# Decode attention on one core: 54 K and V loads moved from SyncE's to GpSimd's queue

## The chip, the cores and the metric

The kernel runs on one core of a Trainium2 chip. The metric is the device time of one execution in microseconds (us), as the median of several runs. The chip's parts go by the profile's names: PE (TensorE, the matrix engine), DVE (VectorE), ACT (ScalarE), POOL (GpSimd) and SP (SyncE, which computes nothing and here issues DMAs). 16 DMA engines move data between the chip's memory and the 128 partitions of the core's own memory.

## The reference

One decoding step of a transformer block for two sequences: layer norm, attention over a cache of 8192 positions with 32 heads of 128, and a gated feed-forward layer, all in bf16.

```python
def _A_ref(x, k_cache, v_cache, wq, wo):      # x: 2 x 1 x 512; caches: 2 x 32 x 8192 x 128
    q = (x @ wq).reshape(B, Sq, Hq, Dh).transpose(0, 2, 1, 3)
    scores = einsum("bhqd,bhkd->bhqk", q, k) * (Dh ** -0.5)
    o = einsum("bhqk,bhkd->bhqd", softmax(scores), v)
    return o.transpose(0, 2, 1, 3).reshape(B, Sq, Hq * Dh) @ wo

def _B_ref(x, W_gate, W_up, W_down):          # F = 1376
    gate, up = x @ W_gate, x @ W_up
    return ((gate * (gate > 0)) * up) @ W_down

h = x + _A_ref(_layernorm(x), k_cache, v_cache, wq, wo)
out = h + _B_ref(_layernorm(h), W_gate, W_up, W_down)
```

Each query meets each key once, so nothing of the caches is used twice: 2 x 2 x 32 x 8192 x 128 elements of 2 B are 268 MB that have to be read.

## The kernel before

**Tiles and steps.** The 64 pairs of sequence and head are worked through two heads at a time, in N = 32 steps. For one step, K of two heads is one tile of 128 partitions by 16,384 elements (ROW; 32 KB a partition, 4 MB in all), and V another. Each partition holds 128 positions (NT) of 128 elements, which lie one after the other in the chip's memory, so that a load is 128 rows of 32 KB, eight for each DMA engine. There are two buffers for K (the halves of kbuf, called kh) and two for V (vbuf); step i uses buffer i % 2 of each.

**A step.** `scores(i)` multiplies K by the query in place on DVE (L358), adds each product row up by halving (L383) and a last reduction (L387), and takes the largest score of each partition (L395), which PE spreads (L397). `powers(i)` runs inside the next step: DVE reduces the largest score (L312) and ACT takes the exponentials into pgz (L315). `values(i)`, also inside the next step, multiplies V by them on PE, two matmuls written out (L408) and the other thirty in a loop that PE runs by itself (L434, L440). ACT collects the result (L450), and PE turns four steps' results at a time (L459).

**Loads.** `load_kv(cache, buf, i, pieces)` issues the load of step i at L144. At the start SP issues, in this order, the weights wq, K of step 0 in four pieces, K of step 1 (K1 below) and V of step 0 (V0). From then on each `scores(i)` with i from 1 to 30 issues K of step i + 1 and then V of step i, behind a `tc.no_sync_barrier()` that sets the order of the plan and waits for nothing by itself. A K load waits until `scores(i - 1)` has read the buffer, a V load until `values(i - 2)` has. SP issues them in order and waits in order. V of step 31, the weights wo, W_gate, W_up and W_down follow on SP as well. The argument `single_packet` asks for all rows that an engine gets of one load to be framed as one packet; before, it is set for i from 1 to 27 (TOGETHER is N - 4 = 28).

**Order.** For four engines the order of instructions is as written; for POOL it is made by a planner:

```python
    ORDERED = {getattr(mybir.EngineType, e) for e in ("PE", "DVE", "Activation", "SP")}
    with tc.manual_schedule(engines=ORDERED):
```

POOL only sets up constants at the start (L174 to L204, the selects through a helper at L151): memsets and selects of ident, pick, nscale, fold, part, quarter, sel, rest and quot. It issues no DMA.

**The end.** Behind the last step come the output projection (L535), the layer norm and the feed-forward layer (L571, L604), and a store of the result (L618).

Of the kernel before, what the change touches and what calls it, by code (L numbers as in the profile page):

```python
# [18 lines left out]
def _dram(t, offset, dims):  # L19
    return bass.AP(tensor=t.tensor, offset=t.offset + offset, ap=[list(d) for d in dims])  # L20
# [3 lines left out]
def kernel(  # L24
# [13 lines left out]
    nc = tc.nc  # L38
# [58 lines left out]
    kh = [kbuf[:, s, :] for s in range(2)]  # L97
# [38 lines left out]
    TOGETHER = N - 4  # L136
# [3 lines left out]
    def load_kv(cache, buf, i, pieces=1):  # L140
        b, g = steps[i]
        w = ROW // pieces
        for k in range(pieces):
            nc.sync.dma_start(  # L144
                out=buf[i % 2][:, k * w:(k + 1) * w],
                in_=_dram(cache, (b * Hkv + 2 * g) * Sk * Dh + k * w, [[ROW, P], [1, w]]),
                single_packet=0 < i < TOGETHER,
            )

    def select(t, fill, base, pattern, mult, op=ALU.not_equal):  # L150
# [13 lines left out]
    with tc.manual_schedule(engines=ORDERED):  # L164

        nc.sync.dma_start(out=wq_all, in_=_dram(A_wq, 0, [[KC * Hq * Dh, P], [1, KC * Hq * Dh]]))  # L166
        for b in range(B):
            nc.scalar.dma_start(out=xrow[b:b + 1, :], in_=_dram(A_x, b * D, [[D, 1], [1, D]]))
        load_kv(A_k_cache, kh, 0, pieces=4)
        load_kv(A_k_cache, kh, 1)  # L170
        load_kv(A_v_cache, vbuf, 0)

        masks.make_identity(nc, ident)
# [473 lines left out]
```

## Time and profile before

| | |
|---|---|
| median of three runs | 659.18 us (659.13 to 659.39) |
| profiled execution | 657.6 us, its span from the first to the last instruction; the profile gives no other time of it |
| busy: PE, DVE, ACT, POOL | 398.7, 607.9, 67.0, 7.9 us |
| DMA | 281.26 MB in 11379 packets, mean 428 GB/s |
| SP's queue (q1) | 11360 packets, 281.06 MB, 99.3% of 16 engines' span |
| first multiply of DVE (L358) | starts at 23.24 us |
| V of step 31 | issued at 614.44 us, landed at 634.45 us |
| last weights | landed at 654.18 us |

How to read it: the page divides the span into 40 slices and gives the busy share of each in tenths; "DMA share" in a table by windows is the mean busy share of the 16 DMA engines. A line of DMA issues gives the KB of one load and the median us from its issue to its landing. In a timeline, "idle before <-releaser" is what the engine waited for. "SPq" is an instruction of SP's queue, "L144" a line of the kernel. Below the page's views the trace keeps a record of each DMA packet, with queue, start, duration and bytes; a packet there is one row of a load, or a 4 B record that ends a load on one engine.

### The profile page before, as it was taken

To read this page: it belongs to the slowest core of one execution; us is meant where nothing else is said; L and a number is where in the kernel's file an instruction comes from. 1 tells how busy PE (TensorE), PEld (TensorE's weight loads), DVE (VectorE), ACT (ScalarE), POOL (GpSimd) and SP (SyncE) were. 2 spreads that over 40 slices of the span, in tenths; PEclk is the share of its full clock that TensorE was granted. 3 is DMA by queue.
4 is the path that set the end of the run, shared out by engine and by line. 5 is a ranking of instruction groups with operands and counts; after the bars stand their busy time and mean duration, and the time that the engine had idled before them with its cause. 6 is when DMAs were issued, how large, how long until landed. Compare 5 with 4: busy or idle time off the path is not lost.

```text
span 657.6 us, 7128 instructions
## 1 busy us (share of the span) xinstructions
PE 398.7 (61%) x1647; PEld 129.5 (20%) x1647; DVE 607.9 (92%) x290; ACT 67.0 (10%) x200; POOL 7.9 (1%) x51
## 2 busy tenths in 40 slices
PE   2127666666676555657666556775556665565496
PEld 1002111211121111211112111121112111121256
DVE  0899999999999999999999999999999999999941
ACT  2110111110000000000000000000000000000220
POOL 4000000000000000000000000000000000000000
PEclk9999788798887777898887789767778876779885
DMA  8999999999999999999999999999999999999997
GB/s 359 439 444 421 442 433 427 444 415 446 427 434 433 427 442 425 440 434 427 440 424 441 429 435 432 429 440 424 440 431 432 438 423 441 432 433 436 425 422 298
DMA packets 11379, 281.26 MB, mean 428 GB/s; under 512 B 1282, under 2 KB 1380, under 8 KB 2020
## 3 DMA queue, kind: packets, MB, share of 16 engines
q1 hardware_dynamic: 11360, 281.06, 99.3%
q8 instruction: 9, 0.15, 0.1%
q14 instruction: 6, 0.05, 0.0%
q10 hardware_dynamic: 4, 0.00, 0.0%
HBM read 281.05 MB, written 0.00 MB: 427 GB/s over the span
## 4 chain that ended last, share of the span: by engine, by line
DVE 61%; DMA 36%; PE 1%; issue 1%; SPq 0%; ACT 0%; DVEq 0%; ACTq 0%
DMA kbuf<-in_A_k_cache_dram 30%; DVE kbuf L358 28%; DVE kbuf L383 27%; DVE scol L387 4%; DMA vbuf<-in_A_v_cache_dram 3%; DMA kbuf<-in_B_W_down_dram 3%; PE po L408 1%; DVE nm L312 1%; DVE pm L395 0%; SPq L144 0%; ACT pgz L315 0%; PE d_ps L604 0%; SPq L166 0%; DVE rz L297 0%; PE y_ps L612 0%
## 5 line engine op out<-in xcount | busy, mean ns | idle before, releaser
L440 PE MATMUL po<-vbuf,pgz 128*8 x870 | 300.1, 443 | 68.0 <-issue 66.7
L358 DVE TENSOR_TENSOR kbuf<-kbuf,qrep 128x16384 bf16<-128x16384 bf16 (+2 forms) x33 | 277.1, 8398 | 10.2 <-DMA kbuf<-in_A_k_cache_dram 9.8
L383 DVE TENSOR_TENSOR kbuf<-kbuf 128x8192 bf16<-128x8192 bf16 (+4 forms) x128 | 274.5, 2144 | 3.3
L440 PEld LDWEIGHTS po<-vbuf,pgz 128*8 x870 | 79.9, 92 | 299.1 <-issue 263.9
L408 PE MATMUL po<-vbuf,pgz 128*8 128x512 bf16 x122 | 47.0, 521 | 135.4 <-PEq L434 111.3
L450 ACT ACTIVATE ob<-po 8x512 f32<-8x512 f32 x31 | 18.2, 586 | 436.5 <-PEq L434 427.3
L387 DVE TENSOR_REDUCE scol<-kbuf 128x128 f32<-128x1024 bf16 (+1 forms) x32 | 38.8, 1214 | 1.2
L315 ACT ACTIVATE pgz<-scol,nm 64x128 bf16<-64x128 f32 x64 | 28.0, 438 | 85.4 <-DVE nm L312 84.5
L397 PE MATMUL mx_ps<-nscale,pm 128*128 128x128 f32 x64 | 15.0, 317 | 29.7 <-DVE pm L395 19.0
L408 PEld LDWEIGHTS po<-vbuf,pgz 128*8 128x8 bf16 x58 | 2.7, 84 | 130.4 <-issue 130.4
L397 PEld LDWEIGHTS mx_ps<-nscale,pm 128*128 128x128 f32 x64 | 9.7, 190 | 39.6 <-issue 19.3
L234 PE MATMUL q_ps<-wbig,xn 128*2 128x512 bf16 x32 | 10.7, 469 | 3.0 <-DMA wbig<-in_A_wq_dram 3.0
L315 ACT ACTIVATION_READ_ACCUMULATOR pgz<-scol,nm 64x1 f32 x64 | 11.7, 184 | 0.0
L312 DVE TENSOR_REDUCE nm<-mx_ps 128x2 f32<-128x128 f32 x32 | 9.1, 284 | 1.4 <-PE mx_ps L397 1.4
L408 PEld LDWEIGHTS <-pgz 128*8 128x8 bf16 x64 | 6.1, 98 | 21.3 <-ACT pgz L315 10.0
L395 DVE TENSOR_REDUCE pm<-scol 128x1 f32<-128x128 f32 x32 | 9.1, 286 | 1.1
L459 PE MATMUL o_ps<-sel,ob 128*128 128x8 f32 (+1 forms) x64 | 8.7, 262 | 0.1
L459 PEld LDWEIGHTS o_ps<-sel,ob 128*128 128x128 f32 x64 | 8.0, 197 | 1.4 <-ACT ob L450 1.2
L215 DVE COPY xc<-x_ps 128x8 f32<-128x8 f32 x1 | 0.2, 167 | 8.4 <-PE x_ps L211 8.4
L238 ACT ACTIVATE qrow<-q_ps 2x512 bf16<-2x512 f32 x8 | 4.7, 587 | 29.5 <-PE q_ps L234 29.5
L242 PE MATMUL r_ps<-qrow,pick 2*64 2x256 bf16 x32 | 3.9, 321 | 5.4 <-ACT qrow L238 5.4
L297 DVE RECIPROCAL rz<-o_ps 128x32 f32<-128x32 f32 (+3 forms) x4 | 1.0, 254 | 5.8 <-PE o_ps L289 4.6
(93 smaller groups left out, 75.5 us busy)
## 6 DMA issues: line engine op xcount, KB each, us to landing
vbuf<-in_A_v_cache_dram SPq DMA_DIRECT2D x32, 4096.0 KB, 23.4
kbuf<-in_A_k_cache_dram SPq DMA_DIRECT2D x31, 4096.0 KB, 19.8
wbig<-in_A_wq_dram SPq DMA_DIRECT2D x1, 4096.0 KB, 12.6
kbuf<-in_A_k_cache_dram SPq DMA_DIRECT2D x4, 1024.0 KB, 17.5
wbig<-in_A_wo_dram SPq DMA_DIRECT2D x1, 2048.0 KB, 24.5
wbig<-in_A_wo_dram SPq DMA_DIRECT2D x2, 1024.0 KB, 26.4
kbuf<-in_B_W_gate_dram SPq DMA_DIRECT2D x1, 1376.0 KB, 31.2
kbuf<-in_B_W_up_dram SPq DMA_DIRECT2D x1, 1376.0 KB
```

Source lines behind the costliest of these rows:

```text
L234: nc.tensor.matmul(out=q_ps[0:B, :], lhsT=xn[:, c, :], rhs=wq_sb[:, c, n * 512:(n + 1) * 512], start=(c == 0), stop=(c == KC - 1),)
L312: nc.vector.tensor_reduce(out=nm, in_=mx_ps, axis=AXIS.X, op=ALU.min)
L315: nc.scalar.activation(out=_free(pgz[s][r, :], j, [[2, NT]]), in_=scol[r, :], func=ACT.Exp, scale=SCALE, bias=nm[r, j:j + 1], accum_out=zc ...
L358: nc.vector.tensor_tensor(out=kv, in0=kv, in1=_free(qrep, (b * NG + g) * Dh, [[0, n], [1, Dh]]), op=ALU.mult,)
L383: nc.vector.tensor_tensor(out=lo, in0=lo, in1=_free(kt, half, [[Dh, nv], [1, half]]), op=ALU.add,)
L387: nc.vector.tensor_reduce(out=scol[:, 0:nv], in_=_free(kt, 0, [[Dh, nv], [1, 8]]), axis=AXIS.X, op=ALU.add,)
L395: nc.vector.tensor_reduce(out=pm, in_=scol, axis=AXIS.X, op=ALU.max)
L397: nc.tensor.matmul(out=mx_ps.rearrange("p a b -> p (a b)"), lhsT=_free(pm, 0, [[0, P]]), rhs=nscale, start=True, stop=True,)
L408: nc.tensor.matmul(out=made[i][0:2 * T4, :], lhsT=pgz[s][:, u * 2 * T4:(u + 1) * 2 * T4], rhs=vbuf[s][:, u * T4 * Dh:(u + 1) * T4 * Dh], s ...
L440: nc.tensor.matmul(out=made[i][0:2 * T4, :], lhsT=pgz[s][:, bass.ds((w * LOOP + u) * (2 * T4), 2 * T4)], rhs=vbuf[s][:, bass.ds((w * LOOP ...
L450: nc.scalar.activation(out=ob[32 * k:32 * k + 2 * T4, :], in_=made.pop(i)[0:2 * T4, :], func=ACT.Copy,)
L459: nc.tensor.matmul(out=o_of(i)[:, 0, 2 * g0:2 * (g0 + n)], lhsT=ob[:, t * Dh:(t + 1) * Dh], rhs=sel[:, t, 0:n, :], start=(t == 0), stop=(t ...
```

## The change

54 of the 64 loads of K and V go to POOL's queue: K of steps 2 to 28 and V of steps 1 to 27. They are the ones with `single_packet` set. The others stay on SP without it: all loads issued at the start, K of steps 29 to 31, V of steps 28 to 31, and all weights. So K1 loses the flag and K28 gains it. Nothing else is changed; buffers, waits and sizes are the same.

```diff
     def load_kv(cache, buf, i, pieces=1):
         b, g = steps[i]
         w = ROW // pieces
+        first = 2 if buf is kh else 1
+        many = first <= i < first + TOGETHER - 1
+        eng = nc.gpsimd if many else nc.sync
         for k in range(pieces):
-            nc.sync.dma_start(
+            eng.dma_start(
                 out=buf[i % 2][:, k * w:(k + 1) * w],
                 in_=_dram(cache, (b * Hkv + 2 * g) * Sk * Dh + k * w, [[ROW, P], [1, w]]),
-                single_packet=0 < i < TOGETHER,
+                single_packet=many,
             )
```

## The prediction

> **What bounds the kernel now.** I read the page first: the busy shares and slices, the queues, the chain that ended last; then the windows by stage, DVE's waits, the SP queue's issues, and last the trace's records of single DMA packets.
>
> ```profile
> DMA  8999999999999999999999999999999999999997
> GB/s 359 439 444 421 442 433 427 444 415 446 427 434 433 427 442 425 440 434 427 440 424 441 429 435 432 429 440 424 440 431 432 438 423 441 432 433 436 425 422 298
> ...
> q1 hardware_dynamic: 11360, 281.06, 99.3%
> ...
> DVE 61%; DMA 36%; PE 1%; issue 1%; SPq 0%; ACT 0%; DVEq 0%; ACTq 0%
> ...
> vbuf<-in_A_v_cache_dram SPq DMA_DIRECT2D x32, 4096.0 KB, 23.4
> kbuf<-in_A_k_cache_dram SPq DMA_DIRECT2D x31, 4096.0 KB, 19.8
> ```
>
> The 16 DMA engines are busy from the first slice to the last, nearly all of it on SP's one queue. The chain's "DVE 61%" must not mislead: up to 247 us DVE works through what the first loads gave it, and after that it waits for K at each step:
>
> ```profile
> core 0: us, PE busy (x) PEld busy (x) DVE busy (x) ACT busy (x) POOL busy (x), PEclk, DMA share, GB/s
> 0.00:43.00 43.00, 9.57 (x34) 3.70 (x34) 25.15 (x16) 6.62 (x10) 7.88 (x51) 1.00 0.98 411
> 43.00:247.00 204.00, 132.12 (x422) 37.98 (x422) 202.12 (x88) 22.69 (x65) 0.00 (x0) 0.85 1.00 432
> 247.00:595.00 348.00, 215.72 (x661) 63.12 (x660) 340.90 (x146) 28.27 (x90) 0.00 (x0) 0.81 1.00 433
> ```
>
> DMA share 1.00 at 432 to 433 GB/s in both middle stages: only a faster packet stream can shorten them. The packet records say how fast it is. Each load is eight rows of 32,768 B per engine; on one engine's sequence, rows follow at 1.2094 us, with 0.006 us more for a record of 4 B that ends the load: 9.681 us, for nearly each of 63 loads. The 8,192 B rows of K's first load follow at 0.3059 us. So 24,576 B more take 0.9035 us, 27.20 B per ns; at that rate 32,768 B need 1.2047 us, and **4.7 ns per row are a fixed cost of each packet**. K1 (flagged as one packet) and V0 (not flagged) both take 9.681 us, so on SP's queue the flag buys nothing.
>
> The cover of an issue is what still runs ahead of it:
>
> ```profile
> start us, us, engine line op out<-in xcount [idle before <-releaser]
> 265.95 0.33 SPq L144 DMA_DIRECT2D kbuf<-in_A_k_cache_dram  x1
> 271.71 0.33 SPq L144 DMA_DIRECT2D vbuf<-in_A_v_cache_dram  x1
> 285.19 0.33 SPq L144 DMA_DIRECT2D kbuf<-in_A_k_cache_dram  x1
> 290.94 0.33 SPq L144 DMA_DIRECT2D vbuf<-in_A_v_cache_dram  x1
> ```
>
> The K load issued at 285.19 has its last row at 305.11, 19.92 us later, of which 9.68 are its own: 10.2 us of work lay ahead of it. The same subtraction over all K and V loads issued from 37.7 us on gives at least 5.35 us (K2, at 37.71), about 10 for K and 14 for V later.
>
> **The change part by part.**
>
> *Issues.* 54 issues of 0.33 to 0.43 us leave SP and 54 appear on POOL, which works only in the first 9.5 us. No issue of POOL is in this trace; the nearest row is SP's 0.33, the far end the 8.1 us for which PE waited on ACT's x loads, but that is transfer in the opening burst and not issue. I bound it at 0.3 to 8 us and take about 1, near SP's row. Anything below 5.35 us is hidden by the rows ahead: cost 0; at 8 us the first loads would come late by up to 2.7 us, once, since from 247 us on K has 10 ahead of it. On POOL, as on SP, a V load queues behind the K load ahead of it, which waits for DVE; nothing else stands behind them there. SP then has K29 and V28 next, whose buffers come free later than those of K28 and V27, so it passes nothing early. The weights follow V31 as now.
>
> *The flag.* K1 loses it and K28 gains it; on SP its worth is 0 (K1 against V0, above).
>
> *Two queues at once.* At 37.7 us K2 on POOL meets V0's last 5.35 us on SP; near 556 us K29 on SP meets V27 on POOL. Work is only reordered. At worst V0 ends behind K2, at 52.7 instead of 43.1 us; its first use is at 49.0 us, so PE starts 4 us late, and V2, which had 9.2 us ahead of it, still has 5. Cost 0; without that cover it would be those 4 us, once.
>
> *The rows themselves.* Here lies the only gain there can be. If GpSimd's queue does frame eight rows as one packet, seven of eight fixed costs go: 7 x 4.7 = 33 ns a load, x 54 = 1.78 us, all on the path, since each load is. Bounds: 0 (as on SP) to all eight and the record at the end, 8 x 4.7 + 6 = 44 ns, x 54 = 2.35 us; below nothing if the queue is worse (rivals). I take 1.78, because that is what one packet for eight rows means. The Trainium skill (DMA: Bandwidth & Descriptors, "Why small descriptors are slow") puts about 3 cycles on each packet, which joining packets saves, and a further 32 B of metadata on each descriptor, which it doesn't; as an estimate that leaves 1.3 us of the 1.78. No run so far shows the split.
>
> *Sum*, against the profiled execution: span 657.6 - 1.8 = 655.8. The three timed runs have a median of 659.18, 1.5 us above that span; the same 1.5 us put the forecast at **657.4 us**, 0.27% faster. A measurement of this kernel tells about 0.2%, or 1.3 us, from no change.
>
> **The rivals.**
>
> *No difference (659.2).* The packet cost stays per row, as SP's flagged loads show it today, and the engines have no idle time to give back. For it: K1 = V0 to the nanosecond. Against: it is another queue. The Trainium skill (same page, "Issuing engines are not separate DMA queues") says that all queues end in the same 16 engines and that issuing from several only saves issue time; by that rule it would be this case, and the busy share of 1.00 agrees with it.
>
> *Slower: the stream loses its perfect packing.* Place: the 54 loads. SP's stream has no gap at all between loads, so GpSimd's can only equal it or be worse there; it decides from 1.32 / 54 = 24 ns a load. Price by the nearest row: if rows are cut to the 8,192 B that K0 has, three more fixed costs a row, 3 x 4.7 x 8 = 113 ns a load, x 54 = 6.1 us: 665.3. Cut in two it would be 2.0 us, 661.2. A stall per load of the kind the trace has where another queue's packet comes between (a row of 1.68 instead of 1.21 us) would be 0.47 x 54 = 25 us, the far end. The Trainium skill (same page, "Measured (HBM→SBUF, 128 partitions, SWDGE, issued from GpSimd)") lists 425 GB/s at 16 MB; at that rate, as an estimate, 54 loads would cost 10 us more.
>
> *Slower: POOL's order.* POOL's instructions are not held in written order, as those of PE, DVE, ACT and SP are; the start shows it, where the memset of quot (written last) precedes the selects of fold:
>
> ```profile
> 3.44 0.10 POOL L186 MEMSET fold<- 128x8 f32 x1
> ...
> 3.68 0.10 POOL L203 MEMSET quot<- 128x4 bf16 x1
> 3.73 0.19 POOL L151 TENSOR_SCALAR_AFFINE_SELECT fold<-fold 128x8 f32<-128x8 f32 x1
> ```
>
> V1's buffer is free from the start. Put ahead of K2, V1 would share the engines with K0, and DVE would start up to 9.7 us late. Then K3 is asked for at 66.4 us, the stream having run dry at 62.4; with about 2 us from issue to first row (the first load: 0.81 to 2.76) 6.0 us are lost for good: 665.2. If V stood ahead of K all the way, K would wait 5.8 us for V's release each step and then behind V's 9.7: some 5 us a step, over 100 us. Against both: a barrier in the source puts the pair behind the earlier step, K first.
>
> *Slower: DVE.* A step's DVE work is 18.8 to 19.0 us of 19.36; 0.34 us to spare. One us more per step over 27 steps would cost about 0.7 x 27 = 18 us, some 677. Nothing in the trace has POOL at work beside DVE's loop. The Trainium skill (SBUF — State Buffer, "Who interferes with whom") says that DVE in a two-port mode keeps GpSimd from writing descriptors, but that tensor_tensor and tensor_reduce did not, and the loop has only these two.
>
> **How the numbers follow.** Forecast 0.40; no difference 0.22; lost packing 0.22; POOL's order 0.10; DVE 0.06. The first is faster, the second the same, the other three slower: 0.38. The range starts at 656.7, just under the largest gain (659.18 - 2.35 = 656.8), and reaches to 667 over both 665 cases; outside are the stall per load, V ahead of K, and a slower DVE. Within the forecast alone it is 656.8 to 657.9.
>
> **What would show it.** Right: a second queue with 54 loads of 4 MB; rows in it at about 1.205 us and loads at 9.65; DMA share still 1.00; K waits of DVE as small as now; V31 landing some 1.8 us earlier than 634.45. No difference: 9.68 again. Lost packing: loads over 9.71 us, or DMA share under 1.00 in the middle stages. POOL's order: first DVE multiply later than 23.24, or V1 issued ahead of K2. DVE: L358 or L383 longer than 8.69 and 4.34 us. The forecast is wrong if loads on GpSimd's queue take 9.68 us or more.

## The result, and the profile after

The changed kernel takes 661.1 us (median of 7 runs, 660.9 to 661.7) against 659.18 us: a ratio of 1.0031, interval 1.0021 to 1.0042. It is 1.9 us slower, where 1.8 us faster was forecast. The profiled execution took 661.43 us with a span of 659.7 us, 2.1 us longer than the span before.

First the page of the changed kernel: the two queues (packets, MB, share of 16 engines' span), the chain by engine, and the issues with KB and median us to landing.

```profile
q0 software_dynamic: 7776, 226.50, 79.6%
q1 hardware_dynamic: 3584, 54.56, 19.4%
...
DVE 7%; PE 3%; issue 0%; DVEq 0%
...
kbuf<-in_A_k_cache_dram POOLq DMA_DIRECT2D x27, 4096.0 KB, 18.5
vbuf<-in_A_v_cache_dram POOLq DMA_DIRECT2D x27, 4096.0 KB, 22.1
```

54 loads are on a queue of their own, as meant. The chain that ended last has changed its kind: it holds only DVE and PE, and it can be followed back only to 589.4 us. Before, its last long wait was the one for the last weights, which landed at 654.18 us. The table by windows shows that the stream itself lost nothing in the middle:

```profile
core 0: us, PE busy (x) PEld busy (x) DVE busy (x) ACT busy (x) POOL busy (x), PEclk, DMA share, GB/s
43.00:247.00 204.00, 130.31 (x418) 37.73 (x418) 201.31 (x87) 22.64 (x65) 10.56 (x20) 0.86 1.00 432
247.00:595.00 348.00, 212.77 (x651) 63.03 (x652) 336.69 (x144) 28.21 (x90) 16.88 (x32) 0.81 1.00 433
```

Share and rate are those of before to the last digit, and the last row of all weights ends at 654.27 instead of 653.93 us. What differs is DVE: 336.7 instead of 340.9 us busy in the second stage. It stood still once. First PE's start on V27, before and after, then DVE's timeline at step 29, before and after:

```profile
568.02 1.01 PE L408 MATMUL po<-vbuf,pgz 128*8 128x512 bf16 x2 [5.14 <-PEq L434]
```

```profile
575.82 1.01 PE L411 MATMUL po<-vbuf,pgz 128*8 128x512 bf16 x2 [11.87 <-DMA kbuf<-in_A_k_cache_dram]
```

```profile
576.37 8.69 DVE L358 TENSOR_TENSOR kbuf<-kbuf,qrep 128x16384 bf16<-128x16384 bf16 x1 [0.25 <-DMA kbuf<-in_A_k_cache_dram]
584.98 0.28 DVE L312 TENSOR_REDUCE nm<-mx_ps 128x2 f32<-128x128 f32 x1
```

```profile
576.74 8.69 DVE L361 TENSOR_TENSOR kbuf<-kbuf,qrep 128x16384 bf16<-128x16384 bf16 x1 [0.25 <-DMA kbuf<-in_A_k_cache_dram]
590.06 0.29 DVE L315 TENSOR_REDUCE nm<-mx_ps 128x2 f32<-128x128 f32 x1 [4.62 <-PE mx_ps L400]
```

PE starts on V27 at 575.82 instead of 568.02 us. The spread of the next maxima (L400) stands behind these matmuls on PE, so DVE's reduction of them waits 4.62 us; before, it did not wait. V27 is late because its load took 30.2 us from issue to landing, where V loads on this queue take 22.1: it landed at 574.3 us, in the kernel before at 566.7, so 7.6 us late. (The wait names a DMA into kbuf, but PE starts 1.5 us after V27's landing, and before it was 1.4 us; what fills that time the trace does not show.) The packet records of one DMA engine tell why. P is a row of V27 on GpSimd's queue, S a row of K29 on SP's, with its start in us:

```
558.22P 559.43P 560.63S 561.84P 563.05S 564.26P 565.47S 566.68P 567.89S 569.10P 570.31S 571.52P 572.73S
```

K29 was issued on SP at 556.84, and its first row on any engine starts at 560.38. From then on each engine gives the queues one row each in turn, although the loads on GpSimd's queue carry single_packet. On this engine five rows of K29 come between those of V27, 6.0 us, and a sixth comes ahead of the record that ends V27's load, another 1.2 us; the rest of the 7.6 us is that the load before it, K28, already landed 0.4 us later. The engines move as much as before; but on one queue all of V27 would have gone first.

How 7.6 us become about 2: PE's spread comes at 589.56 instead of 581.76 us, but before it had been done 2.8 us ahead of the reduction, so DVE is 5.1 us late there. DVE starts its multiply of step 31 at 619.80 instead of 615.10 us (4.7 late), the store is issued at 656.64 instead of 655.44 (1.2 late, since the end of the kernel before spent the rest waiting for weights), and from the store's issue to the end of the span it is 3.1 instead of 2.2 us. So 1.2 us of the profiled 2.1 lie ahead of the store and 0.9 behind it.

### The profile page after: what moved, and what is told of

Its sections match the earlier page's. It is cut to its first block, busy times and chain, and to the rows that moved or that the text cites. A ratio compares the mean times of both kernels' runs of the same rounds, so it can differ in the third digit from the quotient of the medians.

```text
span 659.7 us, 7239 instructions
## 1 busy us (share of the span) xinstructions
PE 398.7 (60%) x1647; PEld 130.1 (20%) x1647; DVE 607.6 (92%) x290; ACT 66.9 (10%) x200; POOL 36.5 (6%) x105
## 3 DMA queue, kind: packets, MB, share of 16 engines
q0 software_dynamic: 7776, 226.50, 79.6%
## 5 line engine op out<-in xcount | busy, mean ns | idle before, releaser
L147 POOL DMA_DIRECT2D kbuf<-in_A_k_cache_dram x27 | 14.4, 534 | 352.4 <-DVE scol L390 311.1
L400 PE MATMUL mx_ps<-nscale,pm 128*128 128x128 f32 x64 | 15.0, 317 | 29.9 <-DVE pm L398 18.8
L147 POOL DMA_DIRECT2D vbuf<-in_A_v_cache_dram x27 | 14.2, 528 | 154.1 <-PEq L437 154.1
L400 PEld LDWEIGHTS mx_ps<-nscale,pm 128*128 128x128 f32 x64 | 9.7, 191 | 39.7 <-PEq L437 19.6
## 6 DMA issues: line engine op xcount, KB each, us to landing
vbuf<-in_A_v_cache_dram POOLq DMA_DIRECT2D x27, 4096.0 KB, 22.1
```

Of the source, the lines that this page charges most:

```text
L147: eng.dma_start(out=buf[i % 2][:, k * w:(k + 1) * w], in_=_dram(cache, (b * Hkv + 2 * g) * Sk * Dh + k * w, [[ROW, P], [1, w]]), single_pa ...
L400: nc.tensor.matmul(out=mx_ps.rearrange("p a b -> p (a b)"), lhsT=_free(pm, 0, [[0, P]]), rhs=nscale, start=True, stop=True,)
```

## The experiments

Theory H says that the time is lost at the handover, where SP takes the loads over while GpSimd's queue still has one to finish; theory Q that each load on GpSimd's queue costs something. Ratios are against the kernel before.

**No handover (e1).** All loads of the loop and the weights go to GpSimd's queue in the old order, and `keep_in_program_order` holds them on POOL in the order as written. The last pair of lines is that of wo; those of W_gate, W_up and W_down are changed in the same way.

```diff
+    def pooled(**kw):
+        tc.keep_in_program_order(nc.gpsimd.dma_start(**kw))
...
-        many = first <= i < first + TOGETHER - 1
-        eng = nc.gpsimd if many else nc.sync
+        many = first <= i
...
-            eng.dma_start(
+            (pooled if many else nc.sync.dma_start)(
...
-                    nc.sync.dma_start(
+                    pooled(
```

> Every load from K2 and V1 on, the weights behind V31 too, goes to GpSimd's queue in the order of before; SP keeps only the opening loads and the store. Theory H (handover): the 1.9 us are lost where the two queues share the engines row by row, when K29 on SP meets V27 on GpSimd's queue at 561 us; with no such meeting the time is that of before, 659.2 us (659.0 to 659.6), and V31 is issued near 614.4 us again. Theory Q (the queue): each load on GpSimd's queue costs 1.92 / 54 = 36 ns; 60 K and V loads and the weights would give 661.3 us or more.

Measured: 659.6 us, ratio 1.0006 (0.9997 to 1.0015). DVE is back in time at step 31:

```profile
615.11 7.62 DVE L363 TENSOR_TENSOR kbuf<-kbuf,qrep 128x14336 bf16<-128x14336 bf16 x1 [0.24 <-DMA kbuf<-in_A_k_cache_dram]
```

So with 93.1% of the stream on GpSimd's queue, where the changed kernel has 79.6%, the loss ahead of the store is gone: the store is issued at 655.40, before at 655.44. Q's 661.3 is out.

**An earlier handover (e2).** V13 meets K15 at about 290 us.

```diff
-        many = first <= i < first + TOGETHER - 1
+        many = first <= i < first + 13
```

> GpSimd's queue keeps only K2 to K14 and V1 to V13; the handover to SP comes at about 290 us. Theory H: V13 lands some 7 us late there, DVE waits once for 4 to 5 us about a step later, and wins back 0.34 us per step in the 16 steps that follow, 5.4 us, so nearly nothing is left at the end: 659.2 to 659.7 us. Theory Q: 26 loads of 36 ns, 0.9 us: 660.1 us.

Measured: 659.45 us, ratio 1.0004 (0.9995 to 1.0013). V13's last packet ends at 300.04, 4.9 us later than the 295.11 of the kernel before; DVE waits once and then is back in step. DVE's waits from 270 to 600 us:

```profile
DVE nm L315 <- PE mx_ps L400: 1.6, 1, 1.6
DVE kbuf L361 <- DMA kbuf<-in_A_k_cache_dram: 1.0, 4, 0.3
```

The delay was smaller than expected (DVE waits 1.6 us, not 4 to 5), and the time is as H has it.

**Four steps earlier (e8).** V23 meets K25.

```diff
-        many = first <= i < first + TOGETHER - 1
+        many = first <= i < first + TOGETHER - 5
```

> GpSimd's queue keeps K2 to K24 and V1 to V23; the handover is V23 against K25, four steps earlier than in the changed kernel. Theory H: the same delay of V23 by some 4 to 7 us and up to 4.6 us of DVE's time, of which 4 x 0.34 = 1.4 us are won back before the end; what is left over the 2 us that the end of the kernel has to spare is 0.5 us: 659.7 us (659.3 to 660.2). Theory Q: 46 loads of 36 ns, 1.6 us: 660.8 us.

Measured: 659.68 us, ratio 1.0008 (0.9999 to 1.0017). It is the cleanest case, because DVE waits as long as in the changed kernel:

```profile
512.14 0.29 DVE L315 TENSOR_REDUCE nm<-mx_ps 128x2 f32<-128x128 f32 x1 [4.64 <-PE mx_ps L400]
```

The same 4.6 us of waiting cost 1.9 us at 590 and 0.4 (interval -0.1 to 1.1) at 512: step 31 starts at 617.97, 2.9 us late instead of 4.7, and the end has that much to spare. The expected time was met, but not as worked out: the store is issued at 655.33, no later than before, and the 0.4 us lie behind it (e9).

**A later handover (e3).** V30 meets V31, one step before the end.

```diff
-        many = first <= i < first + TOGETHER - 1
+        many = first <= i < (N if buf is kh else N - 1)
```

> GpSimd's queue keeps all loads up to K31 and V30; only V31 and the weights are on SP, so the handover is V30 against V31. Theory H: V30 lands some 7 us late, at about 631.8 instead of 624.8 us, and the last matmuls of step 30 (7.6 us) start then; the spread of the last maxima on PE comes at about 639.6, and from there to the end the changed kernel needs 23.3 us: a span of 662.9, time 664.6 us (663.5 to 665.5). Theory Q: 59 loads of 36 ns, 2.1 us: 661.3 us.

Measured: 662.37 us, ratio 1.006 (1.0046 to 1.0074); of the five runs three took 662.1 to 662.4 and two 664.0 and 664.1, and the profile, of a run of 662.12, does not show why. The loss grows as H says, but the median is 2.2 us less than worked out. V30 lands at 630.54, 5.8 us late and not 7; PE starts on it at 630.59, and the maxima follow at 637.58 instead of 639.6 us:

```profile
630.59 7.06 PE L411 MATMUL po<-vbuf,pgz 128*8 128x512 bf16 x24 [12.45 <-DMA vbuf<-in_A_v_cache_dram]
637.58 0.49 PE L400 MATMUL mx_ps<-nscale,pm 128*128 128x128 f32 x2
```

From there the end takes 22.8 us (23.3 were taken).

**Another load hit (e5).** V27 goes to SP, so that K28 is the load that shares.

```diff
-        many = first <= i < first + TOGETHER - 1
+        many = first <= i < TOGETHER + (1 if buf is kh else -1)
```

> V27 goes to SP, everything else as in the changed kernel: one load fewer on GpSimd's queue, and the handover is now K28 (GpSimd's queue) against V27 (SP, issued at about 543 us). Theory H: from about 547.4 us the rows take turns, K28 lands at about 563 instead of 557 us, and DVE waits some 6 us for K in front of the multiply of step 28 instead of 4.6 us for PE inside it; V27 is in time. Step 31 starts 0.3 to 1 us later than in the changed kernel: 661.9 us (661.2 to 662.6). Theory Q: 53 loads of 36 ns: 661.1 us, and no such wait.

Measured: 666.77 us, ratio 1.0116 (1.01 to 1.0131): the right place, far more than expected. K28 had sent at most two rows of eight when the turns began, so nearly all of it shared: it lands at 567.87, not 563, and DVE stands still for K:

```profile
567.89 8.69 DVE L361 TENSOR_TENSOR kbuf<-kbuf,qrep 128x16384 bf16<-128x16384 bf16 x1 [11.13 <-DMA kbuf<-in_A_k_cache_dram]
```

That makes DVE late in giving K28's buffer back. The load of K30 into it is issued at 586.71, when the last row ahead of it had ended at 585.74, and its first row starts at 587.67. The engines stand idle, 3.4 us by the packet records from 550 to 600 us, which no expectation had. One load fewer on the queue, 5.7 us slower than the changed kernel: Q cannot make that.

**Sharing in every step (e6).** All K on SP, V1 to V27 on GpSimd's queue.

```diff
-        many = first <= i < first + TOGETHER - 1
+        many = buf is not kh and first <= i < first + TOGETHER - 1
```

> Only V1 to V27 go to GpSimd's queue; every K stays on SP, so the two queues share the engines in every step. Theory H, with the suspected cost taken 27 times: a K load's first row follows its issue by some 4.5 us, then eight K and eight V rows take turns, 19.4 us, so K lands up to 23.9 us after its issue instead of 19.9 and DVE waits for K in every step, until the engines run empty now and then; 665 to 690 us. Theory Q: 27 loads of 36 ns, 1.0 us: 660.2 us.

Measured: 670.59 us, ratio 1.017 (1.0154 to 1.0185). It lies in the expected range for another reason. In the long middle the sharing costs hardly anything:

```profile
43.00:75.00 32.00, 15.89 (x48) 4.38 (x49) 31.69 (x14) 3.34 (x8) 0.53 (x1) 1.00 0.78 329
75.00:247.00 172.00, 113.86 (x364) 33.27 (x363) 167.55 (x73) 19.50 (x55) 4.75 (x9) 0.82 1.00 433
247.00:550.00 303.00, 186.20 (x566) 53.98 (x566) 296.11 (x129) 24.47 (x79) 7.91 (x15) 0.80 1.00 430
```

The share is 1.00 from 75 to 550 us. It is 0.78 at 43 to 75 us, 6.7 us of idle engines: V1 no longer stands behind K2 on its queue, goes out at once, and takes turns with K0.

```profile
13.05 0.69 POOL L147 DMA_DIRECT2D vbuf<-in_A_v_cache_dram  x1 [3.65 <-issue]
```

DVE's second half of K0 starts only at 33.0 us instead of 23.2, and K3 is asked for at 66.5, when the stream has run dry at 61.6. That is the third rival of the prediction in another kernel, and the 6.0 us worked out for it were near. The other part of the 11.4 us is not taken apart. So H in the form "each meeting costs" falls: a meeting costs where a load that someone waits for was ahead and is not ahead any more.

**The flag (e4, e7).** single_packet off, in the changed kernel and in the kernel before.

```diff
-                single_packet=many,
+                single_packet=False,
```

> The changed kernel with single_packet off everywhere. Theory H: the flag plays no part, since at the handover single rows of both queues take turns although GpSimd's loads carry it: rows at 1.209 us, V27 7 us late, 661.1 us (660.8 to 661.5). Rival F (the flag): without it rows of GpSimd's queue cost more or less; one fixed cost of 4.7 ns on each of 8 rows would be 2.0 us, 659.1 or 663.1 us.

> The kernel before with single_packet off in all loads. Theory H and Q both: the flag does nothing on SP's queue either: 659.2 us (659.0 to 659.5), rows at 1.209 us. Rival F: without it each row pays 4.7 ns more or less, 2.0 us in 54 loads.

Measured: 660.98 us, ratio 1.0029 (1.0019 to 1.004), and 659.17 us, ratio 0.9999 (0.999 to 1.0008). Both are their kernels with the flag. In all four kernels, 98 to 99 of 100 rows of the middle have another row 9.680 to 9.682 us behind them, which is eight rows and the record. In e4 the rows take turns just as well: V27 takes 30.3 us to land, with the flag 30.2. So the flag is worth nothing for the rows on either queue, and nothing for the turns where GpSimd's loads carry it; no load on SP carried it at a handover. Whether the flag joined any rows at all, no trace here shows.

**Two loads only (e9).** K2 and V1 on GpSimd's queue.

```diff
-        many = first <= i < first + TOGETHER - 1
+        many = first <= i < first + 1
```

> GpSimd's queue gets two loads only, K2 and V1; SP takes over with K3 against V1 at about 57 us. It asks what else the queue costs: from the store's issue to the end of the span the kernels on SP's queue alone take 2.2 us, the changed one 3.1, and the other kernels with many loads on GpSimd's queue 2.4 to 3.1. Theory E1 (an end that is longer whenever the queue was used): 2.4 us or more here too, 659.4 to 660.1 us. Theory E2 (it goes with the amount of code and the place where it ends): 2.2 us and 659.2 us. Theory H for the handover: V1 some us late, all of it won back long before the end, no cost.

Measured: 659.3 us against 659.3 us, ratio 1.0002 (0.9992 to 1.0011). The meeting with K3 makes V1's last packet 2.5 us late (63.98 instead of 61.51), without a cost. The store is issued at 655.23 and the span ends at 657.6: 2.4 us, neither 2.2 nor much more.

The traces' last instructions show where the end is longer, in two places. First, SP waits for one semaphore after another at the end, about 0.06 us each. In the kernel before, the one of the store's landing is the last of them; two more stand behind it in e9 and six in the changed kernel. From that wait to SP's sign that it is done it is 0.12, 0.24 and 0.49 us. Second, from that sign to the end of the span it is 0.72 us before, 0.78 in e9 and 1.23 in the changed kernel, where GpSimd's closing instructions take longer; e4 and e5 have 1.24 and 1.10, the other kernels with loads on its queue 0.78 to 0.80. So E1 holds in a small part: two loads on the queue make the end 0.2 us longer. Why GpSimd's closing takes another 0.45 us in the changed kernel stays open.

## Why the prediction was wrong

*The rows themselves* was the term that made the forecast, 7 x 4.7 ns x 54 = 1.78 us. It measured 0. The fixed cost of a row is real, but asking for framing does not take it away: rows on GpSimd's queue have the spacing of SP's, 9.681 us a load, with the flag and without. The row K1 against V0 had said so for SP's queue, and I took the other queue to be better without a row for it. The 1.3 us estimated from the Trainium skill (DMA: Bandwidth & Descriptors, "Why small descriptors are slow") fall with it: that section calls joining worth it only for descriptors of up to 256 B, which the prediction left out, and in no run here does asking for it save anything on rows of 32,768 B.

*Two queues at once* was put at 0. It named both meetings but worked out only the first, K2 against V0, where "work is only reordered" held: K2's first row came at 41.23, when V0's rows were nearly over, and V0's last row ended at 42.23, before at 42.14. For the second, K29 against V27, it worked out nothing; the 14 us that it counts ahead of a V load are cover for a late issue only. A queue of its own changes which load is served next, and V27 itself landed 7.6 us late. DVE was then 5.1 us late at 590 us and still 4.7 at step 31, two steps on. That cost put at 0 measured 1.2 us at the store, 0.6 in e4. The Trainium skill has the rule (DMA: Bandwidth & Descriptors, "Queues, rings and completion order"): each DMA engine goes round its queues packet by packet. The trace agrees, with one row from each queue every 2.42 us, and it shows that a packet here is one row of 32 KB, whatever single_packet says.

*Issues* held: 0.53 us each on POOL, all hidden, and the DMA share stays at 1.00. But the packet times in the prediction, and those worked out from them in the expectations, stand up to 0.9 us late against the profile's clock, on which the landing of a load follows its last packet by some 0.3 us. V0's last row ends at 42.14 there, not 43.06, so K2 had 4.4 us of cover and not 5.35; the shown K load had 9.9 and not 10.2. The first load's first row starts at 1.85, not 2.76, which is 1.0 us after its issue and not 2. The sum does not change by it. *POOL's order* did not come about: K2 goes ahead of V1, and e6 shows what the other order costs. DVE's first multiply starts at 18.50 us, before at 18.41; the 23.24 given as the first is that of K0's second half. *DVE*: its multiply and its first add take 8.69 and 4.42 us as before; no slowing by POOL's issues. *Lost packing* did not come about either. The slower side came from none of the three mechanisms that stood for it.

What stays open is the 0.9 us behind the store. In the kernels with loads on GpSimd's queue the span ends 2.4 to 3.1 us after the store's issue, in the two on SP's alone 2.2. The extra waits of SP make 0.4 us of the 0.9; of the 0.5 in GpSimd's closing only the place is known. In e1, whose store is issued as early as before, the end is 0.5 us longer, and the median 0.4; with a ratio of 1.0006 (0.9997 to 1.0015) such a small cost of the queue is neither shown nor excluded by the times. Of the 2.1 us in the profiled spans, the handover accounts for the 1.2 us ahead of the store. No version run here beats the kernel before.

## What to carry to other kernels

When a saturated stream is split over two queues, ask at each place where both have work which load is now served later, and who waits for it: one queue kept the order in which the loads were needed, two queues shared by rows. Put such a meeting early, where the slack of the steps behind it can win the delay back, or keep the stream on one queue to its end. This stream, whose engines were never idle, could gain only from faster rows, and neither the queue nor the flag made them faster.

## What the runs showed of the hardware

- Between two queues each DMA engine alternates by single rows of 32 KB, starting some 3.5 us after the second queue's issue when the first is busy (556.84 to 560.38 us; 614.93 to 618.52 in e3). With idle engines the first row came 1.0 us after the issue (586.71 to 587.67 in e5).
- single_packet changed the spacing of rows (1.2094 us) on neither queue, nor the turns where GpSimd's loads carried it.
- In the loop an issue of such a load took 0.33 us on SP and 0.53 us on POOL.
